# Another order in the first rounds of an attention and expert kernel: scores in front of v, two masks later, v placed by two engines

## The chip, the cores and the metric

The kernel runs on one core of one Trainium2 chip. Times are device microseconds (us) of one execution. The span of a profile is about 2 us shorter than the time of the same execution. Single executions of one kernel differ by 1 us or more (before: 695.77 to 697.10 us); so times are given with their number and range.

## The reference

```
q, k, v: (4, 8, 768, 64)                         # batch, heads, sequence, head size
scores = q k^T / 8, causal; heads with is_retrieval see everything,
         the others the first 4 keys and the last 64
x = softmax(scores) v                             # reshaped to (3072, 512)
P = exp(x w_gate), 8 rounds of row and column normalisation
out = sum over 8 experts e of P[:, e] * (relu(x w1[e]) w2[e])
```

## The kernel before

Attention is done in 24 units (batch, 256 rows, 4 heads), in one to three *rounds* for each unit (a round is one call of `scores`). Expert 0's two layers are cut into pieces (`fill`) that stand between the rounds, so that TensorE has work while VectorE and ScalarE do the softmax. Then come the other seven experts, in which TensorE does nothing but matmuls. The first rounds are written out by hand; instructions stay on each engine in the order in which they are written here.

```python
def place_v(g):                      # v of block g: raw rows -> PSUM by matmul -> v tile
    for n in range(2):
        t = psA.tile([128, 512], F32, tag="mo", bufs=3)
        ...                          # two matmuls by the identity, 512 columns
        if g == 2: nc.vector.tensor_copy(out=dst, in_=src)
        else:      nc.scalar.activation(out=dst, in_=src, func=AF.Copy, ...)

    keep_warm(blank[:, 0:128], blank, 9)   # 9 matmuls without use
    make_keep(); make_far(); round_first(0)
    make_masks((0,))                 # VectorE, two heads each
    emit_prep(*units[0])             # TensorE transposes k, q; VectorE copies them out: kT
    make_masks((1,))
    round_first(4)
    r0 = scores(0)                   # TensorE
    soften(r0, (0,))                 # ScalarE: exp
    make_masks((2, 3))
    emit_prep(*preps.pop())
    warm(2)                          # 2 more matmuls without use
    place_v(0)
    soften(r0, (1,))                 # VectorE: mask
    sum_later(0)
    r1 = scores(1)
    soften(r1, (0,))
    emit_prep(*preps.pop())
    finish_sums()                    # TensorE: PT v (pv); VectorE: reciprocal (rc), product (xn)
    r2 = scores(2)
    soften(r1, (1,)); soften(r2, (0,))
    warm(2)
    turn()                           # TensorE transposes xn (xt), ScalarE copies it out
    sum_later(1)
    r3 = scores(3)
    place_v(1)
    finish_sums(...)
    ...                              # emit_vfar: VectorE makes vf; turn(); r4 = scores(4)
```

In the views, kT, tr, xn and PT carry the block of 256 rows and the half of the heads in their names (kT_0_1 is the second unit, kT_1_0 the third), sc is a tile of scores, mask_104 to mask_107 are the four pairs of masks.

The first loads are queued by the SP and ScalarE queues (k, q of the first unit, `is_retrieval` as `ret_u`) and by GpSimd's queue (v, k, q of the next blocks, w1 and w2 of expert 0, in this order: v, k, q, v, w1, k, q, v, w2).

The softmax here doesn't subtract the row's maximum and nothing guards it: scores larger than these inputs give would overflow.

## Time and profile before

| | before |
|---|---|
| time, first 3 runs | 696.85 us (695.77 to 697.10) |
| span of the profiled execution | 694.0 us |
| first transposes, first layer's first matmul, second layer's first matmul | 7.20, 20.88, 28.82 us |
| from the second layer's first matmul to the end | 665.2 us |

The head of the page, the busy times of the engines, and the chain of work that ended last:

```profile
span 694.0 us, 16657 instructions
...
PE 680.4 (98%) x6753; PEld 567.4 (82%) x6753; DVE 575.5 (83%) x1163; ACT 422.0 (61%) x775; POOL 158.0 (23%) x183
...
PE 92%; ACT 3%; DVE 3%; issue 1%; POOL 0%; DVEq 0%; ACTq 0%
```

TensorE (PE) is busy 98% and is 92% of the chain. The view by stretches shows where it is not full (each entry is busy us and number of instructions; PEclk is the recorded clock of TensorE, 1.00 is full):

```profile
5.00:10.00 5.00, 2.17 (x24) 1.38 (x24) 4.71 (x13) 4.07 (x8) 5.00 (x7) 0.93 1.57 230
10.00:15.00 5.00, 4.35 (x55) 2.29 (x54) 4.55 (x13) 3.54 (x7) 4.38 (x5) 0.73 1.51 198
15.00:20.00 5.00, 3.79 (x55) 2.29 (x55) 3.73 (x11) 4.72 (x8) 1.26 (x2) 1.00 1.44 196
20.00:30.00 10.00, 9.83 (x152) 7.25 (x150) 8.99 (x24) 6.73 (x9) 4.53 (x5) 1.00 1.76 186
```

TensorE is idle 2.83, 0.65, 1.21 us in the three stretches of 5 us and only 0.17 us in the ten after them. So the opening, to about 20 us, is not TensorE's, and what follows is. VectorE (DVE) is busy 4.71 of 5 and 4.55 of 5 us in the first two stretches.

Lines of TensorE's timeline (start, duration, engine, line, operation, output<-inputs, shapes, count, and in brackets the idle time before and what ended it):

```profile
7.20 0.40 PE L265 MATMUL tr_0_0_174<-ident_93,k_0_0_168 128*128 128x128 f16 x4 [1.92 <-ACT k_0_0_168 L180]
...
9.34 0.61 PE L265 MATMUL tr_0_1_211<-ident_93,k_0_0_168 128*128 128x128 f16 x4
...
12.26 0.50 PE L470 MATMUL sc_0_0_239<-kT_0_1_220 64*128 64x256 f16 x4 [0.33 <-DVE kT_0_1_220 L278]
...
12.88 0.41 PE L271 MATMUL tr_1_0_252<-ident_93,k_0_1_119 128*64 128x128 f16 x8
...
13.45 0.36 PE L307 MATMUL pv_0_0_0_271<-v_0_229,PT_0_0_0_193 128*128 128x65 f16 x6
...
20.88 0.38 PE L377 MATMUL l_436<-xT_76,w_0_124 128*128 128x256 f16 x2
...
28.82 0.59 PE L391 MATMUL l_613<-w_0_131,hT_0_0_0_398 128*128 128x512 f16 x2
```

Four transposes of the same shape take 0.40 us at 7.2 us and 0.61 us at 9.3 us: the clock had fallen to half, as PEclk 0.73 in 10 to 15 us says too. From 12.7 us on it was full again. `l_436` is the first layer's first matmul, `l_613` the second layer's.

Lines of VectorE's timeline:

```profile
4.46 0.17 DVE L222 CAST retf<-ret_u 128x8 f32<-128x8 uint32 x1
...
10.62 0.98 DVE L242 TENSOR_SCALAR mask_107<-keep,over 128x640 f16<-128x640 f16 x2
11.53 0.67 DVE L278 COPY kT_0_1_220<-tr_0_1_211 128x1024 f16<-128x1024 f16 x1
...
13.56 0.69 DVE L278 COPY kT_1_0_269<-tr_1_0_252 128x1024 f16<-128x1024 f16 x1 [0.39 <-PE tr_1_0_252 L271]
...
17.53 0.18 DVE L320 RECIPROCAL rc_0_1_0_354<-pv_0_1_0_346 128x4 f32<-128x4 f32 x1 [1.20 <-PE pv_0_1_0_346 L307]
```

The masks at 10.62 us stand in front of kT_0_1, for which the second unit's scores on TensorE wait (0.33 us, at 12.26). Later there is a wait of 1.20 us for `pv_0_1_0`.

### The profile page before, as it was taken

To read this page: it belongs to the slowest core of one execution; us is meant where nothing else is said; L and a number is where in the kernel's file an instruction comes from. 1 tells how busy PE (TensorE), PEld (TensorE's weight loads), DVE (VectorE), ACT (ScalarE), POOL (GpSimd) and SP (SyncE) were. 2 spreads that over 40 slices of the span, in tenths; PEclk is the share of its full clock that TensorE was granted. 3 is DMA by queue.
4 is the path that set the end of the run, shared out by engine and by line. 5 is a ranking of instruction groups with operands and counts; after the bars stand their busy time and mean duration, and the time that the engine had idled before them with its cause. 6 is when DMAs were issued, how large, how long until landed. Compare 5 with 4: busy or idle time off the path is not lost.

```text
span 694.0 us, 16657 instructions
## 1 busy us (share of the span) xinstructions
PE 680.4 (98%) x6753; PEld 567.4 (82%) x6753; DVE 575.5 (83%) x1163; ACT 422.0 (61%) x775; POOL 158.0 (23%) x183
## 2 busy tenths in 40 slices
PE   7999999999999999999999999999999999999997
PEld 3666766666688888888888888888888888888885
DVE  7886766757999988998898879888898888988785
ACT  6778776764555677775555555655655465555651
POOL 7452320000121231213112221222212222121220
PEclk9999999999999999999999999999999999999999
DMA  9999891001643396427834593359423954245676
GB/s 179 177 184 147 52 82 8 1 2 15 109 77 63 62 147 105 76 54 125 135 61 77 95 150 61 62 88 163 82 51 70 149 101 77 50 75 111 145 158 150
DMA packets 102686, 65.59 MB, mean 95 GB/s; under 512 B 66768, under 2 KB 83152, under 8 KB 102608
## 3 DMA queue, kind: packets, MB, share of 16 engines
q0 software_dynamic: 93408, 57.17, 60.6%
q1 hardware_dynamic: 7552, 6.30, 3.8%
q8 instruction: 53, 0.87, 0.5%
q10 hardware_dynamic: 1648, 1.05, 0.5%
q14 instruction: 25, 0.20, 0.1%
HBM read 52.45 MB, written 6.29 MB: 85 GB/s over the span
## 4 chain that ended last, share of the span: by engine, by line
PE 92%; ACT 3%; DVE 3%; issue 1%; POOL 0%; DVEq 0%; ACTq 0%
PE l1y L762 21%; PE l2y L827 21%; PE l1w L762 10%; PE l2w L827 10%; PE l2z L827 5%; PE l1z L762 5%; PE l1b L742 1%; PE l_3153 L391 0%; PE l_3087 L391 0%; PE l_1496 L391 0%; ACT PT_1_0_0_302 L479 0%; PE l_3069 L391 0%; PE last_10519 L879 0%; PE last_10507 L879 0%; PE l_3229 L391 0%
## 5 line engine op out<-in xcount | busy, mean ns | idle before, releaser
L841 ACT ACTIVATE add<-l2z,Pne 128x256 f32<-128x256 f32 x68 | 28.5, 470 | 74.1 <-PE l2z L827 74.1
L841 ACT ACTIVATE add<-l2w,Pne 128x256 f32<-128x256 f32 x68 | 28.5, 470 | 24.4 <-PE l2w L827 23.6
L377 PEld LDWEIGHTS <-w_0_124 128*128 128x128 f16 x384 | 35.5, 98 | 4.2 <-issue 0.4
L849 POOL DMA_DIRECT2D acc_79<-add x21 | 17.7, 845 | 75.8 <-ACT add L841 38.0
L841 ACT ACTIVATE add<-l2y,Pne 128x256 f32<-128x256 f32 x68 | 28.5, 470 | 10.6 <-PE l2y L827 8.9
L849 POOL DMA_DIRECT2D acc_80<-add x21 | 17.7, 845 | 68.0 <-ACT add L841 25.9
L849 POOL DMA_DIRECT2D acc_82<-add x21 | 17.8, 845 | 67.9 <-ACT add L841 31.1
L849 POOL DMA_DIRECT2D acc_81<-add x21 | 17.7, 849 | 67.5 <-ACT add L841 26.1
L849 POOL DMA_DIRECT2D acc_83<-add x18 | 15.1, 840 | 54.3 <-ACT add L841 23.1
L849 POOL DMA_DIRECT2D acc_84<-add x18 | 15.4, 855 | 45.7 <-ACT add L841 39.6
L762 PEld LDWEIGHTS <-S_6_7761 128*128 128x128 f16 x192 | 18.8, 98 | 2.2
L762 PEld LDWEIGHTS <-S_4_5693 128*128 128x128 f16 x192 | 18.8, 98 | 2.2
L762 PEld LDWEIGHTS <-S_7_8795 128*128 128x128 f16 x192 | 18.8, 98 | 2.2
L762 PEld LDWEIGHTS <-S_5_6727 128*128 128x128 f16 x192 | 18.8, 98 | 2.2
L762 PEld LDWEIGHTS <-S_3_4634 128*128 128x128 f16 x192 | 18.8, 98 | 2.2
L762 PEld LDWEIGHTS <-S_2_3563 128*128 128x128 f16 x192 | 18.8, 98 | 2.2
L844 DVE SCALAR_TENSOR_TENSOR acc_83<-l2y,Pne,acc_83 128x256 f32<-128x256 f32 x38 | 16.6, 478 | 1.3 <-PE l2y L827 1.3
L762 PEld LDWEIGHTS <-S_1_3291 128*128 128x128 f16 x160 | 15.6, 98 | 2.1
L844 DVE SCALAR_TENSOR_TENSOR acc_79<-l2y,Pne,acc_79 128x256 f32<-128x256 f32 x36 | 15.7, 478 | 1.3 <-PE l2y L827 1.3
L844 DVE SCALAR_TENSOR_TENSOR acc_80<-l2y,Pne,acc_80 128x256 f32<-128x256 f32 x36 | 15.7, 478 | 1.3 <-PE l2y L827 1.3
L844 DVE SCALAR_TENSOR_TENSOR acc_82<-l2y,Pne,acc_82 128x256 f32<-128x256 f32 x36 | 15.7, 478 | 1.3 <-PE l2y L827 1.3
L844 DVE SCALAR_TENSOR_TENSOR acc_81<-l2y,Pne,acc_81 128x256 f32<-128x256 f32 x36 | 15.7, 478 | 1.3 <-PE l2y L827 1.3
(2586 smaller groups left out, 2284.8 us busy)
## 6 DMA issues: line engine op xcount, KB each, us to landing
acc_79<-add POOLq DMA_DIRECT2D x21, 256.0 KB, 4.0
acc_80<-add POOLq DMA_DIRECT2D x21, 256.0 KB, 3.2
acc_81<-add POOLq DMA_DIRECT2D x21, 256.0 KB, 3.2
acc_82<-add POOLq DMA_DIRECT2D x21, 256.0 KB, 3.2
acc_83<-add POOLq DMA_DIRECT2D x18, 256.0 KB, 3.3
acc_84<-add POOLq DMA_DIRECT2D x18, 256.0 KB, 9.4
w_0_124<-in_moe_w_dram POOLq DMA_DIRECT2D x1, 1024.0 KB, 11.4
w_0_131<-in_moe_w_dram POOLq DMA_DIRECT2D x1, 1024.0 KB, 17.9
```

The source lines that it names most:

```text
L377: nc.tensor.matmul(out=l1[:, ts(fb % 2, 256)], lhsT=w1[:, dc, ts(fb, 128)], rhs=xT[dc // 2][:, dc % 2, c0:c0 + 256], start=(dc == 0), stop ...
L742: nc.tensor.matmul(out=l1, lhsT=w1[:, dc, ts(fb, 128)], rhs=xT[dc // 2][:, dc % 2, ts(c, CH)], start=(dc == 0), stop=(dc == 3),)
L762: nc.tensor.matmul(out=banks[g, bank][:, f, :], lhsT=lefts1[e][k - 1][:, dc, ts(2 * g + f, 128)], rhs=rights1[c][k - 1][:, dc, :], start=( ...
L827: nc.tensor.matmul(out=banks[bank][q], lhsT=lefts2[e, c][k - 1][:, q, f, :], rhs=rights2[e][k - 1][:, f, :], start=(first and q == 0 and f ...
L841: nc.scalar.activation(out=t[:, q, :], in_=banks[bank][q], func=AF.Copy, bias=0.0, scale=w)
L844: nc.vector.scalar_tensor_tensor(out=dst, in0=banks[bank][q], scalar=w, in1=dst, op0=ALU.mult, op1=ALU.add,)
L849: nc.gpsimd.dma_start(out=acc[c][:, i, n, :, :], in_=t, accum_op=ALU.add)
```

## The change

Its intent: let the scores of the second unit start earlier (two masks out of VectorE's way, v's matmuls behind the scores), and take half of v's copies from ScalarE.

```diff
     def place_v(g):
+        run(gen_place_v(g), 2)
+    def gen_place_v(g):              # both matmul pairs first, then copy, yield, copy
...
-            if g == 2:
+            if g == 2 or n:          # second half by VectorE
                 nc.vector.tensor_copy(out=dst, in_=src)
...
         soften(r0, (0,))
-        make_masks((2, 3))
+        make_masks((2,))
         emit_prep(*preps.pop())
         warm(2)
-        place_v(0)
         soften(r0, (1,))
+        r1 = scores(1)
+        r1[0][0]()
+        place = gen_place_v(0)
+        run(place, 1)
+        r1[1][0]()
         sum_later(0)
-        r1 = scores(1)
-        soften(r1, (0,))
         emit_prep(*preps.pop())
+        run(place, 1)
         finish_sums()
+        make_masks((3,))
         r2 = scores(2)
         soften(r1, (1,))
         soften(r2, (0,))
-        warm(2)
+        place_v(1)
         turn()
         sum_later(1)
         r3 = scores(3)
-        place_v(1)
...
+        r4 = scores(4)
         turn()
-        r4 = scores(4)
```

More of the change, by code (lines that the diff above doesn't have):

```diff
@@ L126, in place_v @@
     def place_v(g):
+        run(gen_place_v(g), 2)
+    def gen_place_v(g):
+        parts = []
         for n in range(2):
@@ L135, in place_v @@
                 )
-            dst, src = v_tile(0)[:, :, 2 * g + n, 0:D], t.rearrange("p (h d) -> p h d", h=H)
-            if g == 2:
+            parts.append((v_tile(0)[:, :, 2 * g + n, 0:D], t.rearrange("p (h d) -> p h d", h=H)))
+        for n, (dst, src) in enumerate(parts):
+            if g == 2 or n:
                 nc.vector.tensor_copy(out=dst, in_=src)
@@ L140, in place_v @@
                 nc.scalar.activation(out=dst, in_=src, func=AF.Copy, bias=0.0, scale=1.0)
+            yield
     def load_v_heads(b, h0, h1):
```

## The prediction

> **What bounds the kernel.** On the page TensorE is busy 680.4 of 694.0 us (98%) and 92% of the chain that ended last. Only the opening is not bound by it: by the stretches view TensorE is idle 6.5 us in the first 20 us and about 0.2 us in 20 to 30 us. The change touches only the first rounds (to about 28 us), so a delay or gain at the end of the opening passes one to one to the end.
>
> In the opening VectorE is the engine that is full: 8.8 to 20.5 us it is idle only twice, 0.39 us before kT_1_0 (waits for transposes of k, q) and 1.20 us before rc_0_1_0 (waits for pv_0_1_0). The chain there alternates: masks, kT_0_1 11.53, scores 12.26, transposes, kT_1_0 13.56, scores, exp PT_1_0_0 14.75 to 16.48, scores, v, pv_0_1_0 17.14, xn, kT_1_1, then vf 19.26, mask of PT_1_0_0 until 20.63, pv_1_0_0.
>
> **What changes** (order of instructions on each engine; durations of the trace, by timeline):
> - Both masks_107 (0.91 us on VectorE) move from 10.62, in front of kT_0_1, to behind xn_0_0: kT_0_1 and the scores of the second unit come 0.9 us earlier (scores about 11.35).
> - v of the first two blocks: of four ScalarE copies (0.49 us apart) two go to VectorE (about 0.61 us each, as the two casts at 31.6 and 32.6 us show): ScalarE -1.0 us, VectorE +1.2 us.
> - Two 512-column warm matmuls (about 0.45 us TensorE, in an idle stretch) go.
> - Scores of round 4 before xt_0_1: those wait for kT_1_1, which VectorE makes before xn; xt no longer holds them. About 0.1 to 0.3 us for TensorE.
> - On the DMA queue the second load of v_1 passes k_1_1 and q_1_1; those are needed at 45 us, so it costs nothing.
>
> **Replay with these durations (an estimate).** The first transposes of round 1 still come behind v's four matmuls and the second unit's scores, on a half-speed clock: TensorE's clock was 0.50 from about 9.3 to 12.7 us. (The Trainium skill, "TensorE: Matmul & The Clock Gate", Part 1, describes a free-running window of about 3.4 us with half or full clock; this trace agrees, 3.4 us.) So kT_1_0 starts at about 13.25 instead of 13.56, and VectorE idles 1 us before it: most of what the mask gave. Then VectorE has v's cast (0.6), before which pv_0_0_0 can't end, so xn_0_0 comes 0.5 us later than before, then the masks (0.9), PT's two masks, another cast (0.6), and kT_1_1 starts at about 18.9 instead of 18.1. The 1.20 us idle vanishes, but it was less than the work brought in. PT_1_0_0 is ready at 21.2 to 21.5 instead of 20.63: 0.5 to 0.8 us later. ScalarE's gain lies off the path. Against that: clock phase differs from run to run, and my half-speed times are rough; a warmer clock gives back up to 0.5 us.
>
> **Prediction.** 697.3 us, about 0.4 us slower, inside the spread of before (695.77 to 697.1); 8 in 10: 695.9 to 698.6. Chances: faster by over 2% 0.005, within 2% 0.99, slower by over 2% 0.005.
>
> **What would show it.** kT_0_1 near 10.6 (step right). kT_1_0 near 13.3, and VectorE idle about 1 us before it. pv_0_0_0's last matmuls wait for the cast. No VectorE idle over 0.3 us from 15 to 20 us. vf near 20.0 instead of 19.26, l1's first matmul near 21.6 instead of 20.88. The same distance at the second layer's first (28.82 before).
>
> **What would make it wrong.** If TensorE is at full clock before 12 us, kT_1_0 moves to 12.7 and the change gains about 0.3 us. Then a gain over 0.35 us would be cut by w2's load, which landed at about 28.5. If the missing warm matmuls leave a window cold, 0.5 to 1.7 us more are lost.

One slip in it: the stretches view gives 6.0 us of idle time of TensorE in the first 20 us, not 6.5.

## The result, and the profile after

After took 698.12 us in the median of 6 runs (697.09 to 699.82), before 696.71 us (695.77 to 697.10, 6 runs). All outputs are right. The ratio is 1.0026, 95% interval 1.0009 to 1.0042: 1.8 us slower in the mean. (A ratio is the mean time of one kernel's runs over the mean of the other's of the same rounds; it is not quite the ratio of the medians.) The second time it ran, beside the experiments, after had a ratio of 1.0007 (0.9993 to 1.0020). So the size itself had to be explained, not only the sign.

The profiled execution of after has a span of 697.5 us, 3.5 us more than before's. Two of its stretches, with the same columns as above:

```profile
10.00:15.00 5.00, 4.21 (x37) 2.16 (x38) 3.91 (x9) 3.10 (x6) 3.16 (x4) 1.00 1.60 193
15.00:20.00 5.00, 3.95 (x48) 2.44 (x45) 3.72 (x11) 2.77 (x5) 1.61 (x2) 1.00 1.35 199
```

TensorE's timeline of after, the groups that answer to those of before:

```profile
8.94 0.61 PE L271 MATMUL tr_0_0_174<-ident_93,k_0_0_168 128*128 128x128 f16 x4 [3.66 <-ACT k_0_0_168 L186]
...
11.61 0.61 PE L271 MATMUL tr_0_1_209<-ident_93,k_0_0_168 128*128 128x128 f16 x4
...
14.75 0.64 PE L277 MATMUL tr_1_0_249<-ident_93,k_0_1_119 128*64 128x128 f16 x8
...
17.20 0.27 PE L313 MATMUL pv_0_0_0_269<-v_0_242,PT_0_0_0_193 128*128 128x65 f16 x2 [1.05 <-DVE v_0_242 L143]
...
24.22 0.38 PE L383 MATMUL l_432<-xT_76,w_0_124 128*128 128x256 f16 x2
...
32.16 0.59 PE L397 MATMUL l_609<-w_0_131,hT_0_0_0_405 128*128 128x512 f16 x2
```

VectorE's timeline of after:

```profile
5.96 0.32 DVE L228 CAST retf<-ret_u 128x8 f32<-128x8 uint32 x1 [1.46 <-DMA ret_u<-in_is_retrieval_dram]
...
12.68 0.69 DVE L284 COPY kT_0_1_218<-tr_0_1_209 128x1024 f16<-128x1024 f16 x1 [0.40 <-PE tr_0_1_209 L271]
...
15.86 0.69 DVE L284 COPY kT_1_0_266<-tr_1_0_249 128x1024 f16<-128x1024 f16 x1 [1.45 <-PE tr_1_0_249 L277]
16.46 0.68 DVE L143 CAST v_0_242<-vp_1_244 128x512 f16<-128x512 f32 x1
17.50 0.18 DVE L326 RECIPROCAL rc_0_0_0_277<-pv_0_0_0_269 128x4 f32<-128x4 f32 x1 [0.36 <-PE pv_0_0_0_269 L313]
```

Read against before:

- The second layer's first matmul comes at 32.16 instead of 28.82 us, 3.34 us later; from there to the end it is 665.3 us (before 665.2). Everything lies in the opening.
- Of this, 1.74 us were there before the change could act: the first transposes started at 8.94 instead of 7.20 us, because the first loads landed late. The value read by `retf` is one of them: it started at 5.96 (before 4.46), when the load of `ret_u` had landed, 5.1 us after its issue (before 3.6). Nothing in front of this point was changed, and in the thirteen other traces of this document the first transposes start between 7.17 and 7.50 us; it is chance.
- Then 1.60 us: from the first transposes to the first layer 15.28 us, before 13.68 us. In this execution TensorE stayed at half clock until about 20 us: four transposes take 0.61 us at 8.9 and at 11.6 us, the group of eight transposes 0.64 us at 14.75 (before 0.41). PEclk says 1.00 there: no clock was recorded before 20 us, and the column shows 1.00 where there is no record. The durations are the better clock.
- The prediction's mechanism is there: pv_0_0_0 waits 1.05 us for `v_0_242`, VectorE's copy of v at 16.46 us.

So this single trace mixes three causes: late loads, the clock, and the order. They need not be independent: the late loads left TensorE without work for 3.66 us in front of the first transposes (before 1.92), and these already ran at half clock (0.61 us against 0.40). The experiments separate the order from the other two.

### The profile page after: what moved, and what is told of

Its sections match the earlier page's. It is cut to its first block, busy times and chain, and to the rows that moved or that the text cites. A ratio compares the mean times of both kernels' runs of the same rounds, so it can differ in the third digit from the quotient of the medians.

```text
span 697.5 us, 16654 instructions
## 1 busy us (share of the span) xinstructions
PE 682.2 (98%) x6751; PEld 568.5 (82%) x6751; DVE 576.3 (83%) x1165; ACT 421.2 (60%) x773; POOL 158.1 (23%) x183
## 3 DMA queue, kind: packets, MB, share of 16 engines
q10 hardware_dynamic: 1648, 1.05, 0.5%
## 4 chain that ended last, share of the span: by engine, by line
PE 92%; ACT 3%; DVE 3%; DMA 1%; issue 1%; DVEq 0%; ACTq 0%
PE l1y L771 21%; PE l2y L836 21%; PE l1w L771 10%; PE l2w L836 10%; PE l2z L836 5%; PE l1z L771 5%; PE l1b L751 1%; DMA ret_u<-in_is_retrieval_dram 1%; PE l_3149 L397 0%; PE l_3083 L397 0%; PE l_1492 L397 0%; PE last_10515 L888 0%; PE last_10503 L888 0%; PE last_10491 L888 0%; PE l_3159 L397 0%
## 5 line engine op out<-in xcount | busy, mean ns | idle before, releaser
L858 POOL DMA_DIRECT2D acc_82<-add x21 | 17.8, 846 | 67.9 <-ACT add L850 31.1
L858 POOL DMA_DIRECT2D acc_80<-add x21 | 17.8, 845 | 67.7 <-ACT add L850 26.0
```

The lines of the kernel that those rows point to most:

```text
L858: nc.gpsimd.dma_start(out=acc[c][:, i, n, :, :], in_=t, accum_op=ALU.add)
```

## The experiments

The distances below are read from each trace: from the first transposes to the first matmul of layer 1 (A) and of layer 2 (B). They don't contain the landing of the first loads. "Half clock" is read from the durations of equal groups and from the clock's records. "Later" is the rest of the span behind the second layer's first matmul.

| kernel | A us | B us | later us | half clock, us of the span | times: mean (range), runs | before beside it: mean, runs |
|---|---|---|---|---|---|---|
| before | 13.68 | 21.62 | 665.2 | 9.3 to 12.7 | 696.51 (695.77-697.10), 6 | |
| after | 15.28 | 23.22 | 665.3 | to 20 | 698.29 (697.09-699.82), 6 | 696.51, 6 |
| after_again | 14.05 | 21.99 | 665.3 | 8.4 to 11.8 | 697.20 (696.38-699.43), 6 | 696.72, 11 |
| after_warm2 | 15.10 | 23.04 | 665.2 | 7.7 to 14.5 | 697.54 (696.70-698.19), 5 | 696.72, 11 |
| after_v_act | 14.32 | 22.26 | 665.2 | 7.5 to 14.3 | 696.49 (695.98-696.91), 5 | 696.72, 11 |
| before_no_warm2 | 14.21 | 22.15 | 666.8 | to 13.5 | 696.55 (695.52-697.80), 5 | 696.72, 11 |
| before_lead | 13.46 | 21.65 | 665.3 | none | 696.03 (695.62-696.40), 5 | 696.50, 9 |
| after_lead | 13.80 | 21.74 | 665.3 | none | 696.25 (696.15-696.42), 5 | 696.50, 9 |
| v_act_lead | 14.17 | 22.11 | 665.7 | 14.4 to 17.8 | 697.26 (696.59-698.52), 5 | 696.50, 9 |
| mask_late_lead | 12.61 | 21.54 | 665.3 | none | 695.95 (695.72-696.08), 5 | 696.50, 9 |
| vfirst_lead | 13.39 | 21.33 | 665.5 | none | 696.27 (696.03-696.78), 5 | 696.29, 11 |
| split_lead | 14.12 | 22.05 | 665.2 | none | 696.48 (696.13-696.90), 5 | 696.29, 11 |
| mask_late_lead_w2 | 12.73 | 20.67 | 665.2 | none | 695.05 (694.81-695.71), 5 | 696.29, 11 |
| before_cold | 16.16 | 24.34 | 665.3 | to 25 | 698.25 (696.76-699.85), 6 | 696.29, 11 |

("None" means none from the first transposes to the last few us of the span; the first warm matmuls run at half clock in all, in mask_late_lead to the end of the lead at about 7.3 us.)

The theories: **V**, VectorE's work in the opening (masks, v's casts) makes the order slower by a fixed amount. **C**, the clock: after leaves TensorE too little to do, and it stays at half clock for longer. Later **P**: the place of v, behind the scores, and not who casts it.

### The same kernel again, and three single parts

**after_again** is after, unchanged.

> The changed kernel once more, for a second trace and more times. Theory V (VectorE): the new order costs 0.8 us at the first layer's first matmul, in every execution; so after minus before is 0.8 us plus chance, about 697.5, and first layer's first matmul comes 0.8 us later after the first transposes than in before (there 20.88 - 7.20 = 13.7 us), so 14.5 us, whatever the clock. Theory C (clock): TensorE, with less to do between 8 and 16 us, doesn't fill a busy stretch of 3.4 us and stays at half clock for longer; then the executions spread (697 to 700 us), and a trace in which four transposes take 0.40 us (full clock) from 12 us on has that distance at 14.5 or less, one in which they take 0.61 us until 20 us has it at 15.3 (as the first trace: 24.22 - 8.94).

TensorE's timeline of this run:

```profile
7.18 0.40 PE L271 MATMUL tr<-ident,k 128*128 128x128 f16 x4 [2.01 <-ACT k L186]
...
12.02 0.41 PE L136 MATMUL vp<-acc,ident 64*64 64x512 f16 x4
...
14.38 0.40 PE L313 MATMUL pv<-v,PT 128*128 128x65 f16 x8 [0.78 <-DVE v L143]
...
21.23 1.03 PE L383 MATMUL l<-xT,w 128*128 128x256 f16 x8
```

VectorE's timeline of this run, from kT_0_1 on:

```profile
10.71 0.69 DVE L284 COPY kT<-tr 128x1024 f16<-128x1024 f16 x1
...
13.04 0.69 DVE L284 COPY kT<-tr 128x1024 f16<-128x1024 f16 x1 [0.60 <-PE tr L277]
13.65 0.68 DVE L143 CAST v<-vp 128x512 f16<-128x512 f32 x1
14.64 0.18 DVE L326 RECIPROCAL rc<-pv 128x4 f32<-128x4 f32 x1 [0.31 <-PE pv L313]
```

The groups here are merged more coarsely (eight masks or matmuls in one line, names without numbers). This time the loads landed as in before and the clock was back at 11.8 us (v's four matmuls in 0.41 us). A is 14.05 us, 0.37 us more than in before. So the order cost 0.4 us in this execution, not 0.8, and the first trace's other 1.2 us (15.28 - 14.05) go with the clock. The wait of pv_0_0_0 for VectorE's cast is 0.78 us. The spread of C is there too: one of six took 699.43 us.

**after_warm2**: the warm matmuls put back.

```diff
         soften(r2, (0,))
+        warm(2)
         place_v(1)
```

> After with the two removed warm matmuls put back, in front of v of the second block. Theory C: the half clock ends earlier more often; the mean falls by 0.5 to 1 us to about 697.3, the spread narrows. Theory V: no effect, or 0.1 us slower; mean stays near 698.1 (ratio to before about 1.002).

Its mean is 697.54 us, 0.3 us over after_again, and not the 0.5 to 1 us less that C had expected; its trace was at half clock from 7.7 to 14.5 us all the same. The range is narrower (to 698.19), but five runs don't prove that. These two matmuls are not what matters for the clock: in this trace they stand at 16.3 us, behind the half clock.

**after_v_act**: both halves of v by ScalarE.

```diff
-            if g == 2 or n:
+            if g == 2:
```

> After, but both halves of v copied by ScalarE again (no cast on VectorE for blocks 0 and 1). Theory V: two casts of 0.6 us leave VectorE's chain, the second half of v is ready about 0.7 us earlier, so 0.8 to 1.2 us faster than after: about 697.0, ratio to before about 1.000. Theory C: the same as after within 0.3 us.

696.49 us in the mean, 0.7 us under after_again; without the one slow execution of after_again (699.43) it is 0.3 us. Its trace had the same half clock as after_warm2's, so these two can be compared: A is 14.32 against 15.10 us, 0.78 us less. That spoke for V (the two also differ by the two warm matmuls).

**before_no_warm2**: before, without its second pair of warm matmuls.

```diff
         soften(r1, (1,)); soften(r2, (0,))
-        warm(2)
         turn()
```

> Before, only without its second pair of warm matmuls. Theory C: 0.5 to 1 us slower than before (697.3 to 697.7) with a wider spread. Theory V: the same as before within 0.2 us.

696.55 us against 696.72 of before: no effect. A is 14.21 us with the half clock lasting to about 13.5. (In this trace 1.6 us more were lost at the very end: from the start of VectorE's last instruction to the end of the span, in which the last store lands, it is 5.6 us, before 4.1. The work in front of that took as long as in before.) C in its first form, that the removed warm matmuls keep the clock down, falls.

### Taking the clock out: a longer lead

In the traces so far the clock was at half, or fell to it, in or just behind the stretches in which TensorE waits for the first loads and for kT_0_0. The Trainium skill, "TensorE: Matmul & The Clock Gate", Part 1, says that the clock is set by activity in a free-running window of 3.4 us, which "doesn't reset when your kernel starts". The traces agree: the half clock lasted 3.4 us in before (9.3 to 12.7), and when it began and ended differed from trace to trace of one and the same order. So the next kernels, from before and after alike, got more matmuls without use in these gaps:

```diff
-        keep_warm(blank[:, 0:128], blank, 9)
+        keep_warm(blank[:, 0:128], blank, 14)
...
         emit_prep(*units[0])
+        keep_warm(blank[:, 0:128], blank, 2)
```

**before_lead**, **after_lead** are before and after with this edit.

> Before with 14 instead of 9 warm matmuls at the start and 2 more between the first transposes and the first scores, so that TensorE has work in the stretches where it waited for the first loads and for kT_0_0. If the half clock is what scatters the opening (theory C), the trace shows full clock from about 6 us on (four transposes of tr_0_1 in 0.40 us, not 0.61), the third kT copy about 0.3 us earlier against the first transposes than in before (13.56 - 7.20 = 6.36), and the mean is 0.2 to 0.5 us under before, about 696.2. Theory V alone: nothing changes.

> After with the same longer lead: the clock is then the same as in before_lead, so what is left between the two is the order alone. Theory V: 0.4 to 0.8 us slower than before_lead, first reciprocal of pv about 0.4 us later against the first transposes. Theory C: no difference to before_lead (within 0.2 us), and the spread of after (696.4 to 699.8) is gone.

TensorE's timeline of before_lead:

```profile
7.18 0.40 PE L265 MATMUL tr<-ident,k 128*128 128x128 f16 x4 [1.18 <-ACT k L180]
...
20.64 1.03 PE L377 MATMUL l<-xT,w 128*128 128x256 f16 x8
```

TensorE's timeline of after_lead:

```profile
7.17 0.40 PE L271 MATMUL tr<-ident,k 128*128 128x128 f16 x4 [0.27 <-ACT k L186]
...
9.31 0.40 PE L271 MATMUL tr<-ident,k 128*128 128x128 f16 x4
...
14.11 0.40 PE L313 MATMUL pv<-v,PT 128*128 128x65 f16 x8 [0.79 <-DVE v L143]
...
20.97 1.03 PE L383 MATMUL l<-xT,w 128*128 128x256 f16 x8
```

Both were at full clock from the first transposes on (tr_0_1's four transposes 0.40 us). A is 13.46 and 13.80 us: **the order alone costs 0.34 us**, the same as the 0.37 us above. The means are 696.03 and 696.25 us, 0.22 us apart, and after_lead's five times lie within 0.27 us. So there is no slow execution of after among these five, and V's sign stays with less than its expected size (0.4 to 0.8 us). before_lead is 0.47 us under before, as C expected, but the interval of that ratio (0.9979 to 1.0004) includes 1. That the time differs by 0.1 us less than A fits the traces: in before_lead the second layer comes 8.19 us after the first (28.83 - 20.64), and in kernels that don't wait 7.94 us. It waited 0.25 us for w2's load; after_lead, which is later, did not.

**before_cold** goes the other way: one warm matmul at the start of before, none later.

```diff
-        keep_warm(blank[:, 0:128], blank, 9)
+        keep_warm(blank[:, 0:128], blank, 1)
...
-        warm(2)                      # both places
```

> Before with one warm matmul at the start and none later, to make the clock late on purpose. Theory C, what half clock costs: four transposes take 0.61 us until 16 us or later, the first layer's first matmul comes 14.5 to 15.3 us after the first transposes (before 13.68), and the time is 0.8 to 1.6 us over before, 697.4 to 698.2, as in the slow executions of after. If the clock costs little (VectorE bounds the opening anyway), 14.2 or less and 697.0 or less.

TensorE's timeline of before_cold:

```profile
7.18 0.61 PE L265 MATMUL tr<-ident,k 128*128 128x128 f16 x4 [5.31 <-ACT k L180]
...
18.99 0.64 PE L271 MATMUL tr<-ident,k 128*64 128x128 f16 x8
...
23.34 1.74 PE L377 MATMUL l<-xT,w 128*128 128x256 f16 x8
```

Half clock until about 25 us, A 16.16 us, and 698.25 us in the mean, 2.0 us over before (ratio 1.0028, 1.0015 to 1.0040). The cost of the clock is larger than expected, and the range, 696.76 to 699.85 us, is that of after. So an opening at half clock is enough to make executions as slow as after's slow ones. That it is the cause in each of those (two of the three at 699.4 us and more have no trace) isn't shown; in the one that has a trace, late loads made up 1.74 us and the clock about 1.2 us.

### The parts of the order, at full clock

**mask_late_lead**: before_lead, with only the masks moved.

```diff
-        make_masks((2, 3))
+        make_masks((2,))
...
         finish_sums()
+        make_masks((3,))
         r2 = scores(2)
```

> Before with the longer lead and only the last two masks made later (behind the first xn), nothing else of the change. Theory V: kT_0_1 0.9 us earlier, but the masks' 0.9 us come back in front of PT_0_1_0, where VectorE of before had idle time of 1.2 us: 0.3 to 0.8 us faster than before_lead, about 695.6, the best of all.

A falls by 0.85 us (13.46 to 12.61), a little more than the 0.3 to 0.8 us by which V expected the time to fall. But the time is 695.95 us, like before_lead's 696.03. TensorE's timeline shows where the gain went:

```profile
7.50 0.40 PE L265 MATMUL tr<-ident,k 128*128 128x128 f16 x4
...
20.11 1.03 PE L377 MATMUL l<-xT,w 128*128 128x256 f16 x8
...
29.04 1.90 PE L391 MATMUL l<-w,hT 128*128 128x512 f16 x8 [0.83 <-DMA w<-in_moe_w_dram]
```

The second layer waited 0.83 us for the load of w2. (The first transposes were 0.3 us late here, since the lead was still running; that is why the distance B gains 0.1 us although the wait ends at 29.04.)

**mask_late_lead_w2** tests this: w2 is queued in front of the third block of v, which is needed only at 31 us.

```diff
-        vraw.append(load_v_pairs(2))
         expw[0] = (expw[0][0], load_w2(0))
+        vraw.append(load_v_pairs(2))
```

> mask_late_lead with the load of w2 of the first expert queued in front of the third block of v (256 KB, needed at 31 us). There TensorE had waited 0.83 us for w2 at 28.2 us. If that wait is what ate the masks' gain, the second layer's first matmul comes at 28.0 to 28.3 instead of 29.04 (8.0 us after the first layer's first, as in kernels that don't wait) and the time falls by 0.6 to 0.9 us to about 695.2, ratio to before about 0.998: better than both kernels. If not, it stays at 696.0.

TensorE's timeline, the first matmuls of the two layers:

```profile
19.96 1.03 PE L377 MATMUL l<-xT,w 128*128 128x256 f16 x8
...
27.90 1.89 PE L391 MATMUL l<-w,hT 128*128 128x512 f16 x8
```

7.94 us from the first layer to the second, without a wait. The mean is 695.05 us, 0.9 us under mask_late_lead; the ratio to before is 0.9982 (0.9970 to 0.9994, mask_late_lead had 0.9991), so it beats both kernels, by 1.2 us over before. By the two ratios, each with before beside it, the step is 0.6 us; in the traces the second layer starts 0.87 us sooner after the first transposes (B). The wait is shown: the gain of the masks was not lost, it was held up by a load. Against before_lead, B is 0.98 us less: 0.25 us of that is before_lead's own wait for w2, and 0.73 us are the masks (A: 13.46 to 12.73).

**split_lead**: before_lead, with only the second half of v of the first two blocks cast by VectorE.

```diff
-            if g == 2:
+            if g == 2 or n:
```

> before_lead with only the split: the second half of each of the first two blocks of v is cast by VectorE. Theory V: VectorE gets 0.6 us in front of the masks of PT_0_0_0 and 0.6 us (less 0.5 of the 1.19 us idle) later: first layer's first matmul 0.5 to 1.0 us later than in before_lead (14.0 to 14.4 after the first transposes, there 13.46), time 696.5 to 697.0. Theory P: the idle time of VectorE takes the casts, 13.5 to 13.7, time as before_lead (696.0).

A rises by 0.66 us (13.46 to 14.12), the time by 0.45 us (696.48 against 696.03; against before beside it the ratio is 1.0002, where before_lead had 0.9992). TensorE's timeline of split_lead has the first layer's first matmul at 21.30 us, with the first transposes at 7.18 as in before_lead. V is right about the split, and P's claim that idle time takes the casts is wrong.

**vfirst_lead**: after_lead, with v's first block in front of the second unit's scores again.

```diff
         warm(2)
+        place_v(0)
         soften(r0, (1,))
         r1 = scores(1)
         r1[0][0]()
-        place = gen_place_v(0)
-        run(place, 1)
         r1[1][0]()
...
-        run(place, 1)
```

> after_lead with the first block of v placed in front of the second unit's scores again (both halves at once), everything else of the change kept, the split over two engines too. Theory P (position): what cost after_lead its gain from the masks was that v came behind the scores, so that pv_0_0_0 waited for its second half (0.79 us); then the first reciprocal comes 0.8 to 1.0 us earlier than in after_lead (6.2 to 6.4 us after the first transposes instead of 7.20), and the first layer's first matmul at 12.7 to 13.1 instead of 13.80. Theory V (the two casts on VectorE): only the place changes, not VectorE's work: 13.5 or more. In both cases the load of w2 holds the second layer until about 28.8 to 29.0, so the time is 696.0 to 696.2 (after_lead 696.2).

The first reciprocal comes at 6.14 us after the first transposes (after_lead 7.20), so 1.06 us earlier: P. But A is 13.39 us, only 0.41 us less, between both expectations. (The time doesn't show even that: the mean is 696.27 us, after_lead's 696.25. It was run at another time. The second layer had been expected to wait for w2 until 28.8 us or later; it started at 28.59, without a wait.) Most of the rest went in one place, the late masks. VectorE's timeline of after_lead has them so:

```profile
15.48 0.67 DVE L248 TENSOR_SCALAR mask<-keep,over 128x640 f16<-128x640 f16 x2
```

VectorE's timeline of vfirst_lead:

```profile
14.49 1.35 DVE L248 TENSOR_SCALAR mask<-keep,over 128x640 f16<-128x640 f16 x2
```

And GpSimd's timeline of vfirst_lead at the same time:

```profile
14.16 1.23 POOL L108 DMA_DIRECT2D q<-in_q_dram  x1 [0.24 <-PE sc L476]
```

The same two masks take 0.67 us in after_lead and 1.35 us in vfirst_lead. In the second, GpSimd's queue was writing a load of q from 14.16 to 15.39 us, over the first 0.9 us of the masks; in the first the load was out (14.05 to 15.28) before the masks began at 15.48. mask_late_lead has the same picture (1.34 us, with a load from 14.29 to 15.64), and so has mask_late_lead_w2 (1.35 us); after and after_again have 0.67 us, with no load being written. In vfirst_lead one of the two masks took 1.06 us, in mask_late_lead 1.05; the others took about 0.38. The Trainium skill, "GPSIMD Engine Reference", 1. Specifications, says that GpSimd's interfaces to SBUF are shared with VectorE; that fits, though no run tested it by itself, and one pair fits less well: in after's trace two masks took 0.67 us from 10.71 us on, although a load was being written from 10.91. Being late, after_lead saved 0.68 us on the masks, which hid most of what v's place costs.

**v_act_lead**: after_lead, both halves of v by ScalarE.

```diff
-            if g == 2 or n:
+            if g == 2:
```

> After with the longer lead and both halves of v copied by ScalarE. Theory V: 0.6 to 0.8 us faster than after_lead (two casts of 0.6 us leave VectorE's chain, ScalarE's second copy costs part of it), about level with before_lead or 0.2 us faster. Theory C: the same as after_lead.

This did not work as a test. Its trace was at half clock from 14.4 to 17.8 us in spite of the lead, and its mean of 697.26 us is 1.0 us over after_lead, against the expectation. One thing can be read before the clock fell: pv_0_0_0's second part started at 14.29 us and had waited 0.91 us for ScalarE, which does the exp of PT_0_1_1 first; in after_lead it waited 0.79 us for VectorE. So at v's place behind the scores, ScalarE is no better at full clock; at half clock it was (0.55 us of waiting in after_v_act against 1.05 us in after_warm2). Why this kernel lost the clock and after_lead didn't isn't tested. The traces give a hint: cut each into stretches of 3.41 us, counted from where its record begins or changes. In the stretch in front of the fall (11.0 to 14.4 us) TensorE was busy 1.77 us, 52%; in after_lead's stretches from 6.2 us on never less than 2.15 us, 63%.

## Why the prediction was right or wrong

The interval held, and the sign of the estimate: 697.3 us predicted (695.9 to 698.6), 698.12 us measured. That the interval held is in part luck: two of the six executions (699.45 and 699.82 us) lie above it, and the order alone, at 0.34 to 0.37 us, would not have brought the median to 1.4 us over before's. The estimate of 0.4 us is close to what the order alone costs, but that it is so close is chance too: it comes from 0.5 to 0.8 us, which was too large, with something taken off for a warmer clock. The chain of reasons was mostly seen, its sizes were not.

- **What bounds the kernel: right.** In all traces but two, the time from the second layer to the end is 665.2 to 665.5 us, whatever was done in front of it.
- **kT_0_1 near 10.6: right** (10.71 in after_again). **kT_1_0 near 13.3**: 13.04, because the clock was back 0.9 us sooner than in before's trace (11.8 instead of 12.7); the prediction had named this chance. VectorE waited 0.60 us for it and not 1 us.
- **pv_0_0_0 waits for the cast, xn 0.5 us later: right.** The wait is 0.78 us, the first reciprocal 0.47 us later (14.64 against 14.17).
- **"PT_1_0_0 is ready ... 0.5 to 0.8 us later": too large.** A is 0.37 us more (0.34 us at full clock). The mis-sized term is the late masks: 0.9 us charged, 0.67 us measured (after_again, 15.74 us), in a stretch in which GpSimd writes no load; and kT_1_0 came 0.2 us earlier than assumed.
- **"If TensorE is at full clock before 12 us, kT_1_0 moves to 12.7 and the change gains about 0.3 us": wrong in its second half.** In after_lead, at full clock, kT_1_0 starts at 12.77 us, and A is still 0.34 us more than before_lead's; the second layer's first matmul comes at 28.91 us, before 28.82. An early kT_1_0 isn't enough, since v's cast and the late masks come behind it.
- **The parts.** At full clock they are: masks later -0.85 us; the split +0.66 us (both measured alone); v behind the scores +0.41 us (measured in the finished order, net of the 0.68 us on the masks). They add to +0.22 us; after_lead is +0.34 us, so 0.12 us are left for the rest of the change and for the parts' effect on each other. Each is read from one trace; mask_late_lead_w2 gives 0.73 us instead of 0.85 for the masks, so 0.1 us is not more than two traces of one order differ by.
- **"A warmer clock gives back up to 0.5 us" as the only word on the clock in the estimate: the step that failed.** The clock and the landing of the first loads are larger than the order. An opening at half clock costs 2.0 us in the mean (before_cold); the prediction had this only among the things that would make it wrong, tied to the missing warm matmuls, and putting those back did nothing.
- **"A gain over 0.35 us would be cut by w2's load": right**, and shown on mask_late_lead: TensorE waited 0.83 us for w2 there, and the masks' gain came out when w2 was queued earlier.

What stays open: whether the changed order itself makes slow executions more frequent. Of 12 runs of after 4 took 698.3 us or more; of 37 runs of before none (the slowest 697.99). That speaks for it, and after_lead had none in 5. But which gap of the order lets the clock fall isn't settled, and late loads can happen to either kernel. In after_warm2 and after_v_act the half clock began at 7.7 and 7.5 us, in front of everything that the change moved, and lasted twice 3.4 us; which suggests that part of the difference between traces is where in the execution the stretches of 3.4 us happen to lie. That is not tested.

## What to carry to other kernels

Before you judge a change in the opening of a kernel by two traces, line them up at the first instruction that waits for a load, and read the clock from the durations of equal matmuls; only the distances behind that point belong to the change. Measure the parts of a reordering one by one with the clock made equal: here one part gained 0.85 us and two others took more than that back. When a part's gain is seen at one point of the trace and missing at the end, look for the next load that lands there; here moving one load turned a gain of nothing into 0.6 us (by the ratios) to 0.9 us.

## What the Trainium skill lacked or had wrong

- "TensorE: Matmul & The Clock Gate", Part 1, gives the window (the traces agree, 3.4 us), but not how busy a window must be for full clock. In before, the stretch that ended with the rise to full clock (about 2.5 to 5.9 us) held matmuls until 5.28 us, so about 80% of it; the stretch of 5.9 to 9.3 us, with about 1.2 us of matmuls (35%), ended in half clock. In after_warm2 the stretch of 7.7 to 11.1 us, with 2.57 us of matmuls (75%), did not bring the full clock back, the next one (3.33 us, 97%) did. The shares are estimates from the timeline, and these few stretches give no threshold.
- The same page, Part 4, says that full clock does not engage for transposes. Here four transposes of 128x128 (`nc.tensor.transpose`) take 0.40 us where the record says full clock and 0.61 us where it says half, so they do run at full clock. Whether they count as activity for the clock, which the page doubts, no run here shows.
- "SBUF — State Buffer", "SBUF: two separate sides", describes a lock between VectorE and GpSimd in which whichever starts first blocks the other, and says how a VectorE operation holds up a load that GpSimd writes. What no page gives is how long such a load holds up a VectorE operation. The traces have a number: with GpSimd's queue writing a load over most of the time, two masks of 128x640 took 1.35 us on VectorE (1.06 us one of them), and 0.67 us with no load being written. That this lock is the reason is not tested.
- "TensorE: Matmul & The Clock Gate", Part 1, warns that the clock's records can be unreliable, but no page says that they can be missing at the start of a profile: after's profile shows 1.00 until 20 us where the matmuls' durations show half clock.
